# When the token numbers are written, and when the last of eight batches is placed, in a Fourier mixing and mixture-of-experts kernel

## The chip, the cores and the metric

The kernel runs on one core of a Trainium2 chip. Its time is the device time of one execution in microseconds, given as the median of three runs. The engines are PE (matrix products), DVE (vector work), ACT (activations and copies), POOL (GpSimd, which here mainly issues the indirect DMAs) and SP, which issues plain loads.

## What is computed

The input is x, 8 batches of 2496 rows of 256 numbers. Each batch is filtered along its rows in the frequency domain; then each of the 19968 rows goes to one of 8 experts, chosen by its logits, and through that expert's two matrices.

```
X = np.fft.rfft(x, axis=1)
F = (filt_r + 1j * filt_i)[None, :, :]
Y = X * F
y = np.fft.irfft(Y, n=x.shape[1], axis=1)
...
logits = x @ w_gate + modality_bias[modality_id]
e_idx = np.argmax(logits, axis=1)
...
for e in range(E):
    mask = e_idx == e
    ...
    h = np.maximum(x[mask] @ w1[e], 0.0)
    out[mask] = gate_w[mask, None] * (h @ w2[e])
```

## The kernel before

The transforms are products with small constant matrices, in three stages for each batch. Stage 3 leaves a batch's filtered rows in an SBUF buffer, yo, as 20 columns (NY) of 128 rows. There are two such buffers (yws, used by batch number modulo 2), so batch g overwrites what batch g-2 left. A row has 256 half-precision numbers, then its token number, then its gate weight.

Routing a batch has four steps. `counting` (line 605) finds each row's expert and counts them, c. `placing` (line 630) writes the token numbers into yo on POOL (line 635), turns the counts into offsets with two matmuls into psO (lines 637 and 638), and computes each row's position, pos_i (line 652). `scatter` (line 674) sends one column of 128 rows to those positions in a DRAM array, bins_d, by an indirect DMA from POOL (line 678): 20 for each batch. `tabling` (line 694) makes the list of blocks of 256 rows of one expert that can now be loaded.

An expert block is loaded by SP (xs, line 756), transposed on PE (pT, line 785) and copied to xT on DVE (line 786). Its expert's w1 is copied on DVE (line 777). Four steps follow, each with a quarter of the first product (line 799, evicted by ACT at line 804) and, for the block before, a quarter of the second (line 812). Then DVE multiplies by the gate weight into osb (line 819; three buffers), and two indirect DMAs from POOL send osb to the rows of out (line 821).

The main loop (line 1136) runs over slots, n. In a slot each batch under way gets a piece of its stages; then `pace` sends some scatters; then expert steps run. Up to slot `end` (87) there are 1.5 steps in a slot; after it, when no stage work is left, four, so one whole block. The last batch's rows are placed in slot 87. The two scatters of an odd slot, and the one of an even slot, become `pace((n - end) % 3)` behind slot 87: one in two of three slots.

PE, ACT and DVE follow a scheduled order that is fixed before the run, and so do the queues of POOL and SP: what stands at a queue's head holds up all behind it. `paced` (line 130) makes an instruction wait for the last matmul in the list marks["pe"] at that point in the program, and so keeps it from being put early in its queue.

Of the kernel before, what the change touches and what calls it, by code (L numbers as in the profile page):

```python
# [16 lines left out]
ALU = mybir.AluOpType  # L17
# [12 lines left out]
def kernel(  # L30
# [12 lines left out]
    nc = tc.nc  # L43

    B, S, D = x.shape
# [31 lines left out]
    DW = D // 2  # L77
# [52 lines left out]
    def paced(ins):  # L130
        tc.add_manual_dep(ins.ins, marks["pe"][-1].name,
                          mybir.DependencyInfo(mybir.DependencyClass.Sync, mybir.DependencyReason.DATA),
                          reason="pace")
# [18 lines left out]
    op = ctx.enter_context(tc.tile_pool(name="opsum", bufs=1, space=bass.MemoryType.PSUM))  # L152
# [34 lines left out]
    NPY = NY // EV  # L187
# [36 lines left out]
    def input_piece(g, k):  # L224

        stage1(g, k)
        if (k + 1) * EV in [t1 for t0, t1 in TCH]:
            load_x()
# [227 lines left out]
    def load_t2(g, c):  # L456
        src = b1_d[g].rearrange("t (jr s) c -> (t jr) s c", jr=4)
        t2 = bp.tile([KB, SCH, D], BF16, tag="t24", name="t2")
        nc.sync.dma_start(t2, src[:, c * SCH:(c + 1) * SCH, :])
        st[g]["t2", c] = t2  # L460

    def load_t4(g, c):
        t0, t1 = TCH[c]
        src = b2_d[g].rearrange("s (jr t) c -> (s jr) t c", jr=4)
        t4 = bp.tile([KA, TCM, D], BF16, tag="t24", name="t4")
        nc.sync.dma_start(t4[:, 0:t1 - t0, :], src[:, t0:t1, :])
        st[g]["t4", c] = t4
# [64 lines left out]
    def stage2(g, k):  # L532

        if k < NK:
            ps = forward(g, k)
        if k > 0:
            pz = inverse(g, k - 1)
        if k < NK:
            filtering(g, k, taken(g, k, ps))
        if k > 0:  # L540
            returned(g, k - 1, pz)
# [88 lines left out]
    def placing(g):  # L630

        yw, lg = st[g]["yw"], st[g]["lg"]
        b3 = [P, NY, E]
        mx, ohT, sc, c = st[g]["route"]
        nc.gpsimd.tensor_single_scalar(yw[:, :, DW:DW + 1], tok, g * S, op=ALU.add)
        psO = pp.tile([P, 2, E], F32, tag="ps")
        nc.tensor.matmul(psO[:, 0, :], lhsT=Lexcl, rhs=c, start=True, stop=True)
        nc.tensor.matmul(psO[:, 1, :], lhsT=ones_sq, rhs=c, start=True, stop=True)
        nc.vector.tensor_sub(lg, lg, mx[:, :, None].to_broadcast(b3))
        nc.scalar.activation(lg, lg, AF.Exp)  # L640
        off = sp.tile([P, E], F32, tag="off")
        nc.vector.tensor_add(off, cnt, ecap)
        nc.vector.tensor_add(off, off, psO[:, 0, :])
        nc.vector.tensor_add(cnt, cnt, psO[:, 1, :])
        yield
        nc.vector.tensor_add(sc, sc, off[:, :, None].to_broadcast([P, E, NY]))
        nc.vector.tensor_mul(sc, sc, ohT)
        yield
        pos = sp.tile([P, NY], F32, tag="pos")
        nc.vector.reduce_sum(pos, sc.rearrange("p e t -> p t e"), axis=AX.X)  # L650
        pos_i = sp.tile([P, NY], I32, tag="posi", bufs=2)
        nc.vector.tensor_copy(pos_i, pos)
        st[g]["pos"] = pos_i
        yield
        ssum = sp.tile([P, NY], F32, tag="ssum")
        nc.vector.reduce_sum(ssum, lg, axis=AX.X)
        nc.vector.reciprocal(yw[:, :, DW + 1].bitcast(F32), ssum)
# [6 lines left out]
    def count(g):  # L664

        run(counting(g))

    def place(g):

        run(placing(g))  # L670
# [3 lines left out]
    def scatter(g, t):  # L674

        rows = P if t < NYF else KA
        with behind("out", 1):
            ins = nc.gpsimd.indirect_dma_start(  # L678
                out=bins_d[:, :], out_offset=IOA(ap=st[g]["pos"][:rows, t:t + 1], axis=0),
                in_=st[g]["yw"][:rows, t, :], in_offset=None)  # L680

        free_of(ins, "bins")
        free_of(ins, "bin_reads")
        tc.add_to_no_dep_group("bins", ins.ins)
        written.append(ins.ins)
        paced(ins)
# [141 lines left out]
    def pad_bins():  # L828

        end = tp_.tile([P, E], F32, tag="end")  # L830
        nc.vector.tensor_add(end, cnt, ecap)
        end_i = tp_.tile([P, E], I32, tag="endi")
        ts(end_i, end, 1.0, 1.0)
        for e in range(E):
            r = nc.values_load(end_i[0:1, e:e + 1], engines=(ET.SP,), min_val=0, max_val=E * CAP - BLK)
            ins = nc.sync.dma_start(bins_d[ds(r, BLK)].rearrange("(p i) w -> p i w", i=NI), pad)
            free_of(ins, "bins")
            free_of(ins, "bin_reads")
            tc.add_to_no_dep_group("bins", ins.ins)
# [61 lines left out]
    opening = []  # L901
    moe = Experts()
    to_bins = []
# [12 lines left out]
    def pace(left):  # L916

        if to_bins and left:
            g, t = to_bins[0]
            if t < NY:  # L920
                scatter(g, t)
                to_bins[0][1] += 1
                left -= 1
            else:
                if g == B - 1:
                    pad_bins()
                opening.append((g, n))
                to_bins.pop(0)
        return left


    def routed(g):

        place(g)
        to_bins.append([g, 0])

    def tabled(g):

        run(tabling(g, KR[g], g == B - 1))
# [8 lines left out]
    with tc.manual_schedule(engines={ET.PE, ET.Activation, ET.DVE}):  # L948
# [92 lines left out]
        tok = const_pool.tile([P, NY, 1], I32)  # L1041
# [36 lines left out]
        def routes(g):  # L1078

            yield from counting(g)  # L1080
            for _ in range(4):
                yield
            yield from placing(g)
            to_bins.append([g, 0])
            yield
            yield from tabling(g, KR[g], False)
# [19 lines left out]
        n = -LONG  # L1106
# [22 lines left out]
    end = begin[B - 1] + OFF3 + NPY + 3  # L1129
    assert opening and not to_bins  # L1130
    n = opening[0][1] + WAIT
# [1 line left out]
    for b in moe.ready:  # L1133
        b["slot"] = 1
    n = 0
    while n <= end or to_bins or opening:
        if n == 0:
            routed(TURNED - 1)
        if n == 4:
            tabled(TURNED - 1)  # L1140
        for g in range(TURNED + 2, B):
            if 0 <= n - begin[g] < NP:
                input_piece(g, n - begin[g])
        for g in range(TURNED + 1, B):
            k = n - begin[g] - OFF2
            if (k + LEAD) % 4 == 0 and 0 <= k + LEAD < NS // EV:
                load_t2(g, (k + LEAD) // 4)
            if 0 <= k <= NS // EV:
                stage2(g, k)
        for g in range(TURNED, B):  # L1150
            k = n - begin[g] - OFF3
            if (k + LEAD) % 3 == 0 and 0 <= k + LEAD < NPY:
                load_t4(g, (k + LEAD) // 3)
            if 0 <= k <= NPY + 1:
                stage3(g, k)
            if k == NPY + 2:
                count(g)
            if k == NPY + 3:
                routed(g)
                tabled(g)  # L1160
        if n <= end:
            pace(pace(pace(3) if n < 8 else 2) if n % 2 or n < GAP else 1)
            owed += STEPS
        else:
            pace((n - end) % 3)
            owed += FT // FQ
        while owed >= 1:
            owed -= 1
            moe.step()
        n += 1  # L1170
# [43 lines left out]
```

## Time and profile before

| | before |
|---|---|
| median of three runs | 594.89 us (594.38 to 596.47) |
| the profiled execution | 592.98 us, with a span of 591.2 us |
| mean granted TensorE clock | 0.941 of full speed |
| share of the span: PE, DVE, ACT, POOL | 87%, 64%, 64%, 62% |

The span is the part of the execution from the first to the last instruction of the profile; all times below count from its start. A busy share is an average over stages that have different limits.

### The profile page before, as it was taken

The numbers are of one execution on the slowest core, as the hardware profiler recorded it, in microseconds if no ns is written. First come the engines' busy times: TensorE is split into PE (matmuls) and PEld (weight loads), VectorE is DVE, ScalarE is ACT, GpSimd is POOL, SyncE is SP. The second block draws the span as 40 slices with busy tenths as digits, with TensorE's granted clock in tenths as the row PEclk, the third lists the DMA queues.
The fourth block names the chain that finished last, engine by engine and source line by source line (L and its number), as shares of the span: only waits on it lengthen the run. The fifth ranks groups of instructions, "written<-read, shape, count | busy, mean of one in ns | idle before, by whom it ended". The sixth has DMA issues, their size and how long they took to land.

```text
span 591.2 us, 16242 instructions
## 1 busy us (share of the span) xinstructions
PE 512.1 (87%) x5115; PEld 463.2 (78%) x5115; DVE 377.6 (64%) x1209; ACT 379.9 (64%) x693; POOL 367.4 (62%) x409
## 2 busy tenths in 40 slices
PE   3689986739969989999999989966999999999991
PEld 2677875628858888888888978855999999999991
DVE  8557986656766777769679777554555555555541
ACT  4578886827856877777876754433666666666660
POOL 8112336727746776774776776777777777655552
PEclk9969998969998998999998999978999999999997
DMA  8949999887697787898667463224444443333321
GB/s 152 184 68 192 197 212 208 180 204 209 160 239 208 203 198 222 231 211 241 184 176 204 139 165 112 87 86 146 137 127 123 119 125 122 118 109 110 99 73 33
DMA packets 69301, 93.29 MB, mean 158 GB/s; under 512 B 11427, under 2 KB 52841, under 8 KB 69059
## 3 DMA queue, kind: packets, MB, share of 16 engines
q0 software_dynamic: 21504, 50.75, 35.2%
q1 hardware_dynamic: 24409, 29.94, 20.1%
q10 hardware_dynamic: 23302, 11.50, 7.4%
q8 instruction: 48, 0.79, 0.6%
q14 instruction: 38, 0.31, 0.2%
HBM read 64.68 MB, written 46.35 MB: 188 GB/s over the span
## 4 chain that ended last, share of the span: by engine, by line
PE 46%; DMA 20%; issue 11%; POOL 9%; DVE 8%; ACT 3%; SPq 0%; POOLq 0%; DVEq 0%; ACTq 0%
PE hps L799 14%; PE ops L812 13%; POOL out_dram L821 5%; DMA t<-b_d 5%; DMA b_d<-t 3%; DMA bins_d<-yo,pos_i 3%; DMA b_d<-z 3%; PE ps L476 3%; DMA out_dram<-osb,meta 2%; DMA g<-g 2%; PE pz L488 2%; PE lt L584 2%; PE ps L569 2%; PE pz L489 2%; PE pT L785 2%
## 5 line engine op out<-in xcount | busy, mean ns | idle before, releaser
L804 ACT ACTIVATE hT<-hps 128x512 f16<-128x512 f32 x316 | 188.1, 597 | 120.7 <-PE hps L799 118.7
L799 PE MATMUL hps<-xT,w 128*128 128x256 f16 x1264 | 203.6, 282 | 5.7 <-DVE xT L786 5.6
L821 POOL DMA_INDIRECT out_dram<-osb,meta x158 | 160.1, 1014 | 76.4 <-DVE osb L819 36.6
L812 PE MATMUL ops<-w2sb,hT 128*128 x1264 | 198.5, 277 | 2.7 <-issue 2.5
L678 POOL DMA_INDIRECT bins_d<-yo,pos_i x160 | 162.1, 1013 | 56.6 <-issue 19.8
L799 PEld LDWEIGHTS <-w 128*128 128x128 f16 x1264 | 148.1, 146 | 11.0 <-DVE xT L786 6.0
L812 PEld LDWEIGHTS <-hT 128*128 128x128 f16 x1264 | 125.2, 99 | 18.9 <-issue 3.1
L819 DVE TENSOR_SCALAR osb<-ops,meta 128x256 f32<-128x256 f32 x158 | 69.4, 475 | 24.9 <-DMA out_dram<-osb,meta 17.3
L777 DVE COPY w<-w1sb 128x2048 f16 x79 | 56.2, 711 | 42.9 <-PE hps L799 41.1
L786 DVE COPY xT<-pT 128x512 f16<-128x512 f16 x79 | 33.4, 423 | 53.0 <-PE pT L785 52.3
L503 ACT CAST xf<-ps 104x512 f16<-104x512 f32 x96 | 56.9, 592 | 11.5 <-PE ps L476 9.5
L510 DVE TENSOR_TENSOR p<-xf,g 104x512 f16<-104x512 f16 x96 | 40.5, 421 | 36.7 <-ACT xf L503 35.8
L525 ACT CAST z<-pz 104x512 f16<-104x512 f32 x72 | 42.5, 590 | 9.7 <-PE pz L489 8.1
L476 PE MATMUL ps<-t,w2m 104*104 104x256 f16 x192 | 39.9, 292 | 8.7 <-DMA t<-b_d 7.9
L511 DVE TENSOR_TENSOR xf<-xf,g 104x512 f16<-104x512 f16 x96 | 40.5, 421 | 10.0 <-DMA g<-g 6.9
L488 PE MATMUL pz<-p,a1m 104*104 104x256 f16 x144 | 37.5, 284 | 2.7 <-DVE p L510 1.8
L218 ACT CAST t<-ps 96x512 f16<-96x512 f32 x52 | 30.1, 581 | 14.3 <-PE ps L214 12.8
L593 DVE COPY yT<-lt 128x512 f16<-128x512 f16 x80 | 33.5, 419 | 7.1 <-PE lt L589 6.3
L489 PE MATMUL pz<-xf,a2m 104*104 104x256 f16 x144 | 36.6, 280 | 0.0
L785 PE MATMUL pT<-ident,xs 128*128 128x128 f16 x316 | 32.8, 227 | 4.4 <-DMA xs<-bins_d 4.4
L144 POOL DMA_DIRECT2D xt<-in_x_dram x32 | 18.3, 573 | 28.7 <-PE fp L253 14.2
L584 PE MATMUL lt<-ident,yo 128*128 128x128 f16 x320 | 31.4, 221 | 3.7 <-ACT z L525 3.3
(206 smaller groups left out, 725.5 us busy)
## 6 DMA issues: line engine op xcount, KB each, us to landing
xs<-bins_d SPq DMA_DIRECT2D x79, 130.0 KB
xt<-in_x_dram POOLq DMA_DIRECT2D x24, 384.0 KB
t<-b_d SPq DMA_DIRECT2D x18, 384.0 KB
t<-b_d SPq DMA_DIRECT2D x15, 416.0 KB
b_d<-z ACTq DMA_DIRECT2D x30, 208.0 KB
b_d<-t ACTq DMA_DIRECT2D x24, 192.0 KB
w1sb<-in_moe_w_dram POOLq DMA_DIRECT2D x16, 256.0 KB
w2sb<-in_moe_w_dram POOLq DMA_DIRECT2D x8, 512.0 KB
```

The lines of the kernel that those rows point to most:

```text
L476: mm = nc.tensor.matmul(ps[:KB, i, :], lhsT=w2m[:, s + i, :], rhs=st[g]["t2", s // SCH][:, s % SCH + i, :], start=True, stop=True)
L488: nc.tensor.matmul(pz[:KB, i, :], lhsT=a1m[:, s + i, :], rhs=p1[:, i, :], start=True, stop=False)
L489: nc.tensor.matmul(pz[:KB, i, :], lhsT=a2m[:, s + i, :], rhs=p2[:, i, :], start=False, stop=True)
L503: nc.scalar.copy(xf, ps[:KB])
L678: ins = nc.gpsimd.indirect_dma_start(out=bins_d[:, :], out_offset=IOA(ap=st[g]["pos"][:rows, t:t + 1], axis=0), in_=st[g]["yw"][:rows, t, ...
L777: cp = nc.vector.tensor_copy(b["w1"].rearrange("p a f -> p (a f)"), w1sb[:, ds(ej, 1)].rearrange("p o a f -> p (o a f)"))
L785: nc.tensor.transpose(pT[:, dc, i, :], xh[:, i, dc * P:(dc + 1) * P], ident)
L799: mm = nc.tensor.matmul(hps[:, k, :], lhsT=b["w1"][:, dc, ft:F:FT], rhs=b["xT"][:, dc].rearrange("p i t -> p (i t)"), start=(dc == 0), sto ...
L804: nc.scalar.activation(b["hT"][:, q * FQ:(q + 1) * FQ, :], hps, AF.Relu)
L812: nc.tensor.matmul(b["ops"][:, i, :], lhsT=b["hT"][:, ft, i * P:(i + 1) * P], rhs=w2sb[:, ds(b["ej"], 1), ft, :], start=(ft == 0 and i == ...
L819: nc.vector.tensor_scalar_mul(osb[:, i, :], b["ops"][:, i, :], gate[:, i, :])
L821: ins = nc.gpsimd.indirect_dma_start(out=out[:, :], out_offset=IOA(ap=b["meta"][:, i, 0:1], axis=0), in_=osb[:, i, :], in_offset=None, bou ...
```

## The change

The token-number write of each batch gets the paced wait. The last batch is placed at slot 89, two slots later, and its scatters then go in three of four slots.

```
@@ -632,7 +632,7 @@
         yw, lg = st[g]["yw"], st[g]["lg"]
         b3 = [P, NY, E]
         mx, ohT, sc, c = st[g]["route"]
-        nc.gpsimd.tensor_single_scalar(yw[:, :, DW:DW + 1], tok, g * S, op=ALU.add)
+        paced(nc.gpsimd.tensor_single_scalar(yw[:, :, DW:DW + 1], tok, g * S, op=ALU.add))
@@ -1133,7 +1133,7 @@
     n = 0
-    while n <= end or to_bins or opening:
+    while n <= end + 2 or to_bins or opening:
@@ -1155,14 +1155,14 @@
             if k == NPY + 2:
                 count(g)
-            if k == NPY + 3:
+            if k == NPY + (3 if g < B - 1 else 5):
                 routed(g)
                 tabled(g)
         if n <= end:
             pace(pace(pace(3) if n < 8 else 2) if n % 2 or n < GAP else 1)
             owed += STEPS
         else:
-            pace((n - end) % 3)
+            pace((n - end) % 4)
             owed += FT // FQ
```

The order of instructions on an engine shows what moves. The first place is POOL's queue where the scatters of batch 4 end and those of batch 5 begin. Here yo_105 is the buffer of the even batches and yo_106 that of the odd ones; the names in brackets are what an instruction waits for, DMASW being the software DMAs that POOL issues itself. Before:

```order
L678 DMA bins_d<-yo_105,pos_i 162048x130 [waits DMASW0_49,PE_49,Activation_49]
L678 DMA bins_d<-yo_105,pos_i 162048x130 [waits DMASW1_49]
L635 TENSOR_SCALAR yo_105<-tok 128x20 [waits DMASW3_49,DMASW4_49,DMASW2_49,DMASW7_49,DMASW1_49,DMASW0_49]
L821 DMA out_dram<-osb,meta 19968x256 [waits DVE_49] x2
L678 DMA bins_d<-yo_106,pos_i 162048x130 [waits DVE_49,PE_49,Pool_49]
```

With the change, in the same place:

```order
L678 DMA bins_d<-yo_105,pos_i 162048x130 [waits DMASW0_49,PE_49,Activation_49]
L678 DMA bins_d<-yo_105,pos_i 162048x130 [waits DMASW1_49]
L635 TENSOR_SCALAR yo_106<-tok 128x20 [waits PE_49]
L821 DMA out_dram<-osb,meta 19968x256 [waits DMASW2_49,DVE_49]
L821 DMA out_dram<-osb,meta 19968x256 [waits DMASW3_49,DVE_49]
```

The write that stands there was that of batch 6, into the buffer that the scatters above it read; it is now that of batch 5, into the other buffer. The DMAs behind it get waits of their own for the DMA eight places ahead, which the old write had covered. The same holds for batches 3, 4 and 6.

The second place is POOL's queue from the last scatters of batch 6 (yo_105) to the first of batch 7 (yo_106). Before:

```order
L678 DMA bins_d<-yo_105,pos_i 162048x130 x5
L821 DMA out_dram<-osb,meta 19968x256 x4
L678 DMA bins_d<-yo_106,pos_i 162048x130 x3
L821 DMA out_dram<-osb,meta 19968x256 x2
L678 DMA bins_d<-yo_106,pos_i 162048x130
```

With the change:

```order
L678 DMA bins_d<-yo_105,pos_i 162048x130 x5
L821 DMA out_dram<-osb,meta 19968x256 x4
L635 TENSOR_SCALAR yo_106<-tok 128x20
L821 DMA out_dram<-osb,meta 19968x256 x2
L678 DMA bins_d<-yo_106,pos_i 162048x130
L821 DMA out_dram<-osb,meta 19968x256 x2
L678 DMA bins_d<-yo_106,pos_i 162048x130
```

The write of batch 7 arrives here, from the place ahead of batch 6's scatters, and the three scatters in a row are gone.

The third place is DVE's queue where batch 7 is placed and tabled. Before:

```order
L727 SCALAR_TENSOR_TENSOR bj<-bj,done,jio 128x25
L777 ISA
L777 COPY w_8407<-w1sb 128x2048
L819 TENSOR_SCALAR osb<-ops,meta 128x256 x2
L775 TENSOR_LOAD ej_i
L775 ISA x2
L786 COPY xT<-pT 128x512
```

With the change:

```order
L819 TENSOR_SCALAR osb<-ops,meta 128x256
L725 TENSOR_REDUCE bj<-m 128x25
L819 TENSOR_SCALAR osb<-ops,meta 128x256
L727 SCALAR_TENSOR_TENSOR bj<-bj,done,jio 128x25
L777 ISA
L777 COPY w_8405<-w1sb 128x2048
L775 TENSOR_LOAD ej_i
L775 ISA x2
L786 COPY xT<-pT 128x512
```

The copy of w1 and two steps of the table, which stood ahead of the fourth multiply into osb after the counts, now stand between its halves or behind it. On PE the two psO matmuls move behind one more block; ACT's order stays.

## Rows read from the trace of the kernel before

**Rows 1.** The page, busy time (share of the span) and instructions of each engine.

```profile
PE 512.1 (87%) x5115; PEld 463.2 (78%) x5115; DVE 377.6 (64%) x1209; ACT 379.9 (64%) x693; POOL 367.4 (62%) x409
```

**Rows 2.** Stages: length, busy PE, PEld, DVE, ACT, POOL (instructions), clock, DMA share, GB/s.

```profile
364.00:383.00 19.00, 19.00 (x216) 17.59 (x215) 11.25 (x34) 10.12 (x17) 14.54 (x15) 1.00 0.28 85
383.00:412.00 29.00, 18.54 (x133) 15.23 (x132) 14.64 (x52) 9.07 (x16) 22.03 (x23) 0.82 0.36 112
425.00:507.00 82.00, 82.00 (x790) 77.26 (x789) 44.73 (x111) 52.22 (x88) 63.03 (x62) 1.00 0.42 126
```

**Rows 3.** Waits of DVE from 364 to 430: total us, times, longest.

```profile
DVE osb L819 <- DMA out_dram<-osb,meta: 17.3, 8, 5.5
```

**Rows 4.** Timeline of PE, 380 to 500: start, duration, instruction [idle before <-releaser].

```profile
381.65 0.39 PE L785 MATMUL pT<-ident,xs 128*128 128x128 f16 x4
...
388.80 0.60 PE L637 MATMUL psO<-c,Lexcl 128*128 128x8 f32 x2 [5.33 <-DVE c L627]
...
401.28 0.66 PE L799 MATMUL hps<-xT,w 128*128 128x256 f16 x4 [1.18 <-DVE xT L786]
...
409.37 1.07 PE L799 MATMUL hps<-xT,w 128*128 128x256 f16 x4 [3.94 <-DVE xT L786]
...
425.44 0.38 PE L785 MATMUL pT<-ident,xs 128*128 128x128 f16 x4
...
496.59 0.39 PE L785 MATMUL pT<-ident,xs 128*128 128x128 f16 x4
```

**Rows 5.** Timeline of POOL, 224 to 405, at the token-number writes and a later pair.

```profile
224.38 0.74 POOL L635 TENSOR_SCALAR yo<-tok 128x20 int32<-128x20 int32 x1 [4.36 <-DMA bins_d<-yo,pos_i]
...
268.61 1.05 POOL L678 DMA_INDIRECT bins_d<-yo,pos_i  x1 [0.30 <-PE ps L214]
276.06 0.32 POOL L635 TENSOR_SCALAR yo<-tok 128x20 int32<-128x20 int32 x1 [6.41 <-DMA bins_d<-yo,pos_i]
...
277.47 1.30 POOL L821 DMA_INDIRECT out_dram<-osb,meta  x1 [0.30 <-DVE yT L593]
...
316.63 0.91 POOL L678 DMA_INDIRECT bins_d<-yo,pos_i  x1 [0.30 <-issue]
320.25 0.28 POOL L635 TENSOR_SCALAR yo<-tok 128x20 int32<-128x20 int32 x1 [2.72 <-DMA bins_d<-yo,pos_i]
...
359.51 1.33 POOL L678 DMA_INDIRECT bins_d<-yo,pos_i  x1 [0.30 <-issue]
363.74 0.28 POOL L635 TENSOR_SCALAR yo<-tok 128x20 int32<-128x20 int32 x1 [2.89 <-DMA bins_d<-yo,pos_i]
...
404.07 1.00 POOL L821 DMA_INDIRECT out_dram<-osb,meta  x1 [0.30 <-issue]
```

**Rows 6.** Timeline of DVE: one multiply, and the positions of batches 5 and 6.

```profile
271.66 0.47 DVE L819 TENSOR_SCALAR osb<-ops,meta 128x256 f32<-128x256 f32 x1
...
315.53 0.17 DVE L652 CAST pos_i<-pos 128x20 int32<-128x20 f32 x1
...
355.79 0.17 DVE L652 CAST pos_i<-pos 128x20 int32<-128x20 f32 x1
```

**Rows 7.** Timeline of DVE, 384 to 410.

```profile
384.67 0.88 DVE L819 TENSOR_SCALAR osb<-ops,meta 128x256 f32<-128x256 f32 x2 [4.41 <-DMA out_dram<-osb,meta]
...
401.53 0.31 DVE L727 SCALAR_TENSOR_TENSOR bj<-bj,done,jio 128x25 f32<-128x25 f32 x1
...
407.95 0.88 DVE L819 TENSOR_SCALAR osb<-ops,meta 128x256 f32<-128x256 f32 x2 [5.51 <-DMA out_dram<-osb,meta]
...
409.33 0.68 DVE L777 COPY w<-w1sb 128x2048 f16 x1
```

**Rows 8.** Timelines: POOL's last scatter, SP's load behind it, PE's transposes of that block.

```profile
500.74 0.92 POOL L678 DMA_INDIRECT bins_d<-yo,pos_i  x1 [0.30 <-PE pT L785]
...
503.15 0.33 SPq L756 DMA_DIRECT2D xs<-bins_d  x1
...
519.15 0.39 PE L785 MATMUL pT<-ident,xs 128*128 128x128 f16 x4
```

More of the change, by code (lines that the diff above doesn't have):

```diff
@@ L634, in placing @@
         mx, ohT, sc, c = st[g]["route"]
-        nc.gpsimd.tensor_single_scalar(yw[:, :, DW:DW + 1], tok, g * S, op=ALU.add)
+        paced(nc.gpsimd.tensor_single_scalar(yw[:, :, DW:DW + 1], tok, g * S, op=ALU.add))
         psO = pp.tile([P, 2, E], F32, tag="ps")
@@ L1135 @@
     n = 0
-    while n <= end or to_bins or opening:
+    while n <= end + 2 or to_bins or opening:
         if n == 0:
@@ L1157 @@
                 count(g)
-            if k == NPY + 3:
+            if k == NPY + (3 if g < B - 1 else 5):
                 routed(g)
@@ L1164 @@
         else:
-            pace((n - end) % 3)
+            pace((n - end) % 4)
             owed += FT // FQ
```

## The prediction

> **What bounds the kernel now.** I read the page first, then the stages, then the three engines that meet in the worst stage. The page gives PE 87% of the span and POOL 62% [rows 1]; a mean like this hides that POOL is the limit in one stretch. In the windows, PE is busy for 82 of 82 us from 425 on, but for only 18.5 of 29 us between 383 and 412, with a granted clock of 0.82 there [rows 2]. Just before, from 364 to 383, POOL issues 15 instructions in 19 us, and 23 in the next 29 us: one every 1.26 us, with nothing free between them.
>
> The waits say who holds whom: DVE's multiply into osb (line 819) waits 17.3 us in eight pieces for scatters into out [rows 3]. osb has three buffers, so block k needs the landing of block k-3's two scatters, and those stand in POOL's queue behind the scatters into the bins. PE then waits for what is queued behind line 819 on DVE: 5.33 us for the counts c, later 1.18 and 3.94 us for xT [rows 4].
>
> How much is lost? In the undisturbed part 19 blocks, by their transposes, take 496.59 - 425.44 = 71.15 us, 3.74 us each. The seven blocks from 381.65 to 425.44 take 43.79 us where 7 x 3.74 = 26.2 would do, plus 0.9 for the two psO matmuls: **16.7 us lost** [rows 4]. That is the most that this stretch can give back.
>
> Why is POOL so late? At each token-number write (line 635) it stands still until the scatters just ahead in its own queue have landed: 6.41, 2.72 and 2.89 us before the writes at 276.06, 320.25 and 363.74 [rows 5]. It was reading ahead: the write for batch g stood one batch early, directly behind the last scatters of the buffer that it overwrites.
>
> **The change, part by part.**
>
> *The tied write.* The eight writes stay, 0.3 us each. They now stand just ahead of their own batch's scatters and wait for PE alone, as the first pieces of the order show. By then their buffer's scatters have landed long ago, since stage 3 has overwritten that buffer. So the three stalls go. What POOL finds next decides how much of each is kept:
> - Batch 4. POOL is free of the last scatter at 268.61 + 1.05 = 269.66. The next scatter into out needs osb, which DVE finishes at 271.66 + 0.47 = 272.13 [rows 6]; so it goes out at about 272.5 in place of 277.47 [rows 5]. Kept: 5.0 of the 6.41 us.
> - Batch 5. The last scatter ahead ends at 317.54 [rows 5], now 312.5. The write, two scatters into out (2.6 us) and gaps lead to about 316.2. That batch's positions are ready at 315.53 + 0.17 = 315.7 [rows 6], so POOL doesn't wait for them. Kept: 2.72 less some 0.3 for the write's own gap, 2.4.
> - Batch 6. The same sum: 2.89 less 0.2, and positions are ready at 355.96 [rows 6] against a first scatter near 357. Kept: 2.7.
>
> Together POOL runs 5.0 + 2.4 + 2.7 = **10.1 us earlier** from about 357 on. It does not fall idle in between: the positions come 0.3 to 1 us ahead of it. The paced wait is for a matmul ahead of psO, which the positions need anyway, so it is over earlier still.
>
> There is a new wait to price: in the order each scatter now also waits for the software DMA eight places ahead. The slowest landing seen is from 268.61 to 276.06, 7.45 us [rows 5], and eight places take 8 x 1.26 = 10.1 us. I take nothing; the lower bound is nothing, the upper one the 2.7 us of one short stall.
>
> The Trainium skill, DMA: Bandwidth & Descriptors, section Anatomy of one DMA — SWDGE (gpsimd) path, prices a DMA from this queue at about 2.0 us fixed plus bytes over 436 GB/s. For a scatter of 128 rows of 520 bytes that is an estimate of 2.15 us; three such waits less their gaps would make a lead of 5.6 us, less the 1.3 us below a gain of 4.3, and 590.6 us at the end. The rows above show up to 7.45 us under load, so I keep them.
>
> *Placing two slots later.* PE's two psO matmuls move behind one more block, and with them DVE's steps from line 643 on. The work is the same. Before, PE stood 5.33 us at psO for c [rows 4], because c stood on DVE behind the line 819 that waited for a landing until 384.67 [rows 7]. That landing now comes at 384.67 - 10.1 = 374.6, before DVE needs it near 380.3 (384.67 less its 4.41 us of waiting). So this stall goes through POOL's lead alone, and the move is cover on top. It also carries a cost: in the order of the change DVE's placing and tabling steps crowd around the multiply that is late next. Lines 725, 727 and the w1 copy (line 777) now stand between that multiply and the next xT copy. I take 0.31 us, line 727's, for each of the two steps and 0.68 for the copy [rows 7], 1.3 us in all; nothing is the lower bound.
>
> *Three per four.* Behind the write, batch 7's first three scatters no longer stand in one row ahead of a pair for out; one does. From there on POOL has 11 issues in four blocks (8 out, 3 bins) in place of 8 in three. Between 425 and 507 it issued 62 in 82 us, 1.32 us each [rows 2]: 11 x 1.32 = 14.5 us, against 4 x 3.74 = 14.96 us of PE. It fits, narrowly. Batch 7's last scatter moves one block later, 3.74 us against PE. Before, it is issued at 500.74, the load that waits for it at 503.15, and PE takes up that block at 519.15 [rows 8]: 16 us of cover, some 10 left after the move and a POOL that lags 2 us more. Price nothing; without cover each microsecond late would count in full.
>
> **The sum.** What is late next is the same multiply as before, the one at 407.95 [rows 7], since the pair that frees its buffer stands behind nine bin scatters that the change doesn't move. This pair goes out at 404.07 - 10.1 = 394.0 and lands, 3.88 us after its issue as before, at 397.85. PE would like to go on at 383.5 + 3 x 3.74 + 0.9 = 395.6 (383.5 being half a block behind the transposes at 381.65), so a wait remains. Before, PE resumed at 409.37, 1.42 us behind that multiply's start; now at 397.85 + 1.42 + 1.3 = 400.6. **Gain: 409.37 - 400.6 = 8.8 us.** Behind it the next multiplies are due near 402, 408 and 412. The pairs that they need are issued from 394.0 on at 2.6 us a pair, with the write or one scatter between, and land near 401, 404 and 408. From 509 on nothing changes in size. The half-speed matmuls after the one remaining stall stay in both traces. The profiled execution took 592.98 us; less 8.8 that is 584.2. The median, 594.89, is 1.9 us above it, so I predict 594.89 - 8.8 = **586.1 us**.
>
> **The rivals.** About 0.3% (1.8 us) is what a measurement here can tell from no change.
> - *Everything comes back.* If POOL's lead reached 15 us, no multiply would wait: 594.9 - 16.7 = 578.2. For it: there is also a stall of 4.36 us at 224.38 [rows 5], which I count at nothing, because the work between 225 and 276 had time to absorb it. Against it: the positions of batches 5 and 6 are ready only 0.3 to 1 us before POOL wants them, which caps the lead. Gain over 12 us: chance 0.10.
> - *A smaller lead.* POOL's pitch is 1.26 us while DVE stands waiting and 1.32 us while DVE works [rows 2]. If the freed DVE slows POOL between 357 and 397, 30 issues cost 30 x 0.06 = 1.8 us, and if half of batch 4's gain is lost to pacing, 2.5 more: gain 4.6, time 590.3. The Trainium skill, SBUF — State Buffer, section Who interferes with whom, has a rule that points this way: VectorE and GpSimd share a pair of ports, and a copy in a two-port mode blocks GpSimd's descriptor writing until it ends. Gain 2 to 5 us: chance 0.09.
> - *No effect.* If only the last stall counts, 2.7 less the 1.3 on DVE gives 1.4 us, 593.5: chance 0.08.
> - *Slower: POOL becomes the bound of the tail.* The place is the 22 blocks over which batch 7 is scattered. It decides from a pitch of 14.96 / 11 = 1.36 us on; each 0.1 us above that costs 1.1 us in four blocks, 6 us in all. To end slower than before the pitch must pass 1.36 + (8.8 + 1.8) / 60 = 1.54; at 1.60 the cost is 5.5 x 11 x 0.24 = 14.5 us and the time 594.9 - 8.8 + 14.5 = 600.6. Against it: 1.32 was measured with the same mix. Chance 0.05.
> - That the write does not move is excluded by the order.
>
> **How the numbers follow.** The forecast, a gain of 5 to 12 us, has the remaining 0.68, its own range 583 to 590. The range to hold 8 in 10 runs from inside the first rival to inside the second: 580.5 to 591.5 us. Faster by over 0.3%: 0.68 + 0.10 + 0.09 = 0.87; same 0.08; slower 0.05.
>
> **What would show it.** Right: no idle time of several us before line 635 on POOL; the wait of 5.33 us at psO gone; the scatters of batch 6 start near 357; one stall of PE near 396 to 401, with line 819 waiting for a scatter into out near 397.9; the transposes 3.74 us apart from about 410 to the end. Wrong: POOL idle before line 635 for PE, or before scatters for a software DMA or for positions (then the lead is smaller); a pitch over 1.36 us after 410 with line 819 waiting again; PE waiting for xs near 510. If PE's loss between 380 and 420 is still over 14 us, the step from POOL's lead to the landing is wrong.

## The result, and the profile after

The changed kernel takes 588.1 us, the median of four runs (586.75 to 589.24); the kernel before took 595.47 us in the runs beside it. The ratio is 0.9876, with a 95% interval of 0.9846 to 0.9905: 7.4 us faster, where 8.8 us and 586.1 us were predicted. The profiled execution of after is one of 589.24 us, with a span of 587.4 us.

The page's line of busy times, to be read against [rows 1]:

```profile
PE 507.8 (86%) x5115; PEld 460.9 (78%) x5115; DVE 376.2 (64%) x1209; ACT 379.7 (65%) x693; POOL 370.1 (63%) x409
```

Nothing in it has moved by more than a point. The windows of the same stretches as in [rows 2] say more (columns as there):

```profile
364.00:383.00 19.00, 19.00 (x223) 17.69 (x222) 13.09 (x44) 10.15 (x17) 14.65 (x15) 1.00 0.28 85
383.00:412.00 29.00, 24.11 (x217) 21.56 (x215) 16.89 (x60) 14.06 (x25) 22.58 (x23) 0.94 0.41 132
...
425.00:507.00 82.00, 82.00 (x789) 77.09 (x787) 44.89 (x111) 52.11 (x88) 63.23 (x62) 1.00 0.40 123
```

Between 383 and 412 PE now issues 217 instructions where it issued 133, with a granted clock of 0.94 in place of 0.82. POOL's 23 issues are the same: it is as full as before, but it is further on in its list. (Batch 6's psO comes 4.3 us later in this trace, as shown below; a window moved by as much, 387.3 to 416.3, has PE busy for the same 24.11 us.) The total of DVE's waits for scatters into out, to be read against [rows 3], falls from 17.3 us in eight pieces to this:

```profile
DVE osb L819 <- DMA out_dram<-osb,meta: 5.7, 2, 4.5
```

The timeline of POOL at the token-number writes and at what follows them, against [rows 5]:

```profile
273.70 0.29 POOL L635 TENSOR_SCALAR yo<-tok 128x20 int32<-128x20 int32 x1
...
276.37 1.06 POOL L821 DMA_INDIRECT out_dram<-osb,meta  x1 [2.38 <-DVE ni L705]
277.74 1.07 POOL L678 DMA_INDIRECT bins_d<-yo,pos_i  x1 [0.30 <-issue]
...
315.93 0.35 POOL L635 TENSOR_SCALAR yo<-tok 128x20 int32<-128x20 int32 x1
...
321.40 0.98 POOL L678 DMA_INDIRECT bins_d<-yo,pos_i  x1 [1.95 <-issue]
...
358.39 0.28 POOL L635 TENSOR_SCALAR yo<-tok 128x20 int32<-128x20 int32 x1
...
361.47 0.98 POOL L678 DMA_INDIRECT bins_d<-yo,pos_i  x1 [0.31 <-PE ps L572]
...
398.73 1.00 POOL L821 DMA_INDIRECT out_dram<-osb,meta  x1 [0.30 <-DVE m L723]
400.04 0.99 POOL L821 DMA_INDIRECT out_dram<-osb,meta  x1 [0.30 <-issue]
...
499.37 0.91 POOL L678 DMA_INDIRECT bins_d<-yo,pos_i  x1 [0.30 <-PE hps L799]
```

None of these writes has idle time ahead of it. Two earlier ones, of batches 0 and 2, have, 1.50 us at 83.23 and 3.03 us at 166.86, both for PE, which the prediction had named as a sign of a smaller lead; but the scatter into out behind the second goes out at 167.68, and before it went out at 168.55. Two short idle times stand elsewhere, 2.38 us before a scatter into out and 1.95 us before batch 5's first scatter. DVE's timeline shows what they are for:

```profile
275.61 0.48 DVE L819 TENSOR_SCALAR osb<-ops,meta 128x256 f32<-128x256 f32 x1
...
320.45 0.17 DVE L652 CAST pos_i<-pos 128x20 int32<-128x20 f32 x1
```

The first is the wait for osb that the prediction counted: the multiply ends at 276.09. For the second the profile names no releaser, but that scatter reads batch 5's positions, and these are ready at 320.62, 0.78 us before it starts. In the second trace of the changed kernel, reported below, it again starts 0.78 us behind them (315.96 to 316.74, with 1.87 us idle). The rows at 398.73 and 400.04 are the pair that [rows 5] shows with its first half at 404.07. PE, against [rows 4]:

```profile
355.15 0.39 PE L637 MATMUL psO<-c,Lexcl 128*128 128x8 f32 x2 [0.78 <-DVE c L627]
...
397.12 0.66 PE L799 MATMUL hps<-xT,w 128*128 128x256 f16 x4 [0.91 <-DVE xT L786]
...
405.22 1.07 PE L799 MATMUL hps<-xT,w 128*128 128x256 f16 x4 [3.98 <-DVE xT L786]
...
408.41 0.39 PE L785 MATMUL pT<-ident,xs 128*128 128x128 f16 x4
412.14 0.38 PE L785 MATMUL pT<-ident,xs 128*128 128x128 f16 x4
...
498.31 0.38 PE L785 MATMUL pT<-ident,xs 128*128 128x128 f16 x4
```

The 5.33 us at batch 7's psO are gone. One stall of 3.98 us remains, with 0.91 us a block ahead of it. From 408.41 on the transposes stand 3.75 us apart: 24 blocks take 89.90 us. The timeline of DVE at the two multiplies that still wait, against [rows 7]:

```profile
393.67 0.88 DVE L819 TENSOR_SCALAR osb<-ops,meta 128x256 f32<-128x256 f32 x2 [1.24 <-DMA out_dram<-osb,meta]
...
402.90 0.48 DVE L819 TENSOR_SCALAR osb<-ops,meta 128x256 f32<-128x256 f32 x1 [4.46 <-DMA out_dram<-osb,meta]
```

**A measure that compares executions.** Absolute times don't compare well here: batch 6's psO starts at 350.83 in the trace before and at 355.15 after. Most of what follows is read from the **stretch**, the time from the start of that psO to the end of the span, and from two points counted from the same psO: the **pair**, the first of the four scatters into out behind batch 6's last five (398.73 above), and the **restart** of PE behind its longest late stall (405.22 above). The **lead** is how much earlier the pair stands than in the two executions of before, 52.6 us on average. All columns but the last are from one profiled execution in each row.

| kernel | span | psO of batch 6 | stretch | pair | lead | time, or ratio to before |
|---|---|---|---|---|---|---|
| before | 591.2 | 350.83 | 240.4 | 53.2 | | 595.47 |
| before again | 586.9 | 346.41 | 240.5 | 52.0 | | 588.76 (one run) |
| after | 587.4 | 355.15 | 232.3 | 43.6 | 9.0 | 0.9876 [0.9846, 0.9905] |
| after again | 580.5 | 350.52 | 230.0 | 43.1 | 9.5 | 582.36 (one run) |
| write tied only | 585.6 | 350.66 | 234.9 | 44.4 | 8.2 | 0.9908 [0.9869, 0.9947] |
| placing and cadence only | 591.7 | 350.87 | 240.8 | 52.6 | 0.0 | 1.0009 [0.9975, 1.0043] |
| changed, write tied in batch 5 only | 590.1 | 352.12 | 238.0 | 51.5 | 1.1 | 591.97 (one run) |
| changed, write tied in 6 and 7 only | 584.7 | 351.58 | 233.1 | 46.4 | 6.2 | 586.54 (one run) |
| tied and later, old cadence | 588.6 | 352.79 | 235.8 | 45.0 | 7.6 | 0.981 [0.9733, 0.9887] |
| before, four osb | 587.3 | 347.45 | 239.9 | 56.9 | -4.3 | 0.9979 [0.9944, 1.0014] |
| after, four osb | 578.3 | 348.11 | 230.2 | 44.9 | 7.7 | 0.9707 [0.963, 0.9783] |

The ratios leave out the slower of a kernel's executions where they spread: the one of "after, four osb" rests on three of six runs and the one of the old cadence on two of four, and the traces of the old cadence and of the changed kernel on the slower chip (below) are of executions that are left out.

### The profile page after: what moved, and what is told of

Same layout as the page of the kernel before. It is cut to its first block, busy times and chain, and to the rows that moved or that the text cites. A ratio compares the mean times of both kernels' runs of the same rounds, so it can differ in the third digit from the quotient of the medians.

```text
span 587.4 us, 16253 instructions
## 1 busy us (share of the span) xinstructions
PE 507.8 (86%) x5115; PEld 460.9 (78%) x5115; DVE 376.2 (64%) x1209; ACT 379.7 (65%) x693; POOL 370.1 (63%) x409
## 4 chain that ended last, share of the span: by engine, by line
PE 51%; DMA 17%; issue 10%; DVE 8%; POOL 7%; ACT 4%; SPq 1%; DVEq 0%; POOLq 0%; ACTq 0%
PE hps L799 16%; PE ops L812 15%; DMA b_d<-t 5%; POOL out_dram L821 5%; DMA t<-b_d 4%; PE ps L476 2%; PE ps L569 2%; PE lt L584 2%; DMA g<-g 2%; PE pz L488 2%; PE pT L785 2%; PE ps L572 2%; PE pz L489 2%; PE ps L214 1%; DMA g<-in_filt_i_dram 1%
## 5 line engine op out<-in xcount | busy, mean ns | idle before, releaser
L678 POOL DMA_INDIRECT bins_d<-yo,pos_i x160 | 164.4, 1027 | 68.2 <-issue 21.7
L821 POOL DMA_INDIRECT out_dram<-osb,meta x158 | 161.5, 1022 | 71.8 <-DVE osb L819 34.7
L476 PE MATMUL ps<-t,w2m 104*104 104x256 f16 x192 | 39.2, 287 | 10.1 <-DMA t<-b_d 9.3
L569 PE MATMUL ps<-t,wbm 96*128 96x256 f16 x120 | 30.6, 284 | 4.9 <-DMA t<-b_d 4.8
```

The costliest lines, as they stand in the source:

```text
L476: mm = nc.tensor.matmul(ps[:KB, i, :], lhsT=w2m[:, s + i, :], rhs=st[g]["t2", s // SCH][:, s % SCH + i, :], start=True, stop=True)
L678: ins = nc.gpsimd.indirect_dma_start(out=bins_d[:, :], out_offset=IOA(ap=st[g]["pos"][:rows, t:t + 1], axis=0), in_=st[g]["yw"][:rows, t, ...
L821: ins = nc.gpsimd.indirect_dma_start(out=out[:, :], out_offset=IOA(ap=b["meta"][:, i, 0:1], axis=0), in_=osb[:, i, :], in_offset=None, bou ...
```

## The experiments

**The tied write alone.** The first hunk of the change, nothing else.

```
-        nc.gpsimd.tensor_single_scalar(yw[:, :, DW:DW + 1], tok, g * S, op=ALU.add)
+        paced(nc.gpsimd.tensor_single_scalar(yw[:, :, DW:DW + 1], tok, g * S, op=ALU.add))
```

> Only the token-number write is tied to its placing; the last batch is placed where it was, at two scatters in three blocks. Theory (POOL's lead does it): the three standstills of POOL before line 635 go, the 5.33 us wait at psO shrinks to under 1 us although psO has not moved, and nearly the whole gain is here: 588 us, 586.5 to 590. Rival (the later placing does it, as cover for the counts): the stall at psO stays at 3 us or more and the time is 593 to 596.

Measured: 587.25 us against 593.27. Its timeline of PE shows four idle pieces between 380 and 420:

```profile
383.76 0.39 PE L637 MATMUL psO<-c,Lexcl 128*128 128x8 f32 x2 [0.99 <-DVE c L627]
...
393.43 0.66 PE L799 MATMUL hps<-xT,w 128*128 128x256 f16 x4 [1.22 <-DVE xT L786]
...
401.08 1.07 PE L799 MATMUL hps<-xT,w 128*128 128x256 f16 x4 [3.43 <-DVE xT L786]
...
416.09 0.66 PE L799 MATMUL hps<-xT,w 128*128 128x256 f16 x4 [1.72 <-DVE xT L786]
```

The psO wait shrinks from 5.33 to 0.99 us without the later placing. So it does go through POOL's lead. The last piece, 1.72 us, is one that after doesn't have; it comes after the three scatters of batch 7 in one row.

**The later placing and the new cadence, without the tied write.**

```
-    while n <= end or to_bins or opening:
+    while n <= end + 2 or to_bins or opening:
...
-            if k == NPY + 3:
+            if k == NPY + (3 if g < B - 1 else 5):
...
-            pace((n - end) % 3)
+            pace((n - end) % 4)
```

> Only the last batch's placing two slots later, and three scatters in four blocks; the write is not tied. Theory: the 5.33 us wait at psO goes, but PE then waits for the same multiply into osb, whose buffer is freed at about 408 as before; POOL still stands still before line 635; time 594.5 us, 593 to 596. Rival (later placing does it): 588 to 590 us.

Measured: no difference, 593.46 us against 593.27. POOL's timeline still has the idle time before its writes; three rows of it, and PE's two longest stalls:

```profile
274.68 0.33 POOL L635 TENSOR_SCALAR yo<-tok 128x20 int32<-128x20 int32 x1 [6.56 <-DMA bins_d<-yo,pos_i]
...
319.33 0.34 POOL L635 TENSOR_SCALAR yo<-tok 128x20 int32<-128x20 int32 x1 [4.00 <-DMA bins_d<-yo,pos_i]
...
363.39 0.52 POOL L635 TENSOR_SCALAR yo<-tok 128x20 int32<-128x20 int32 x1 [2.50 <-DMA bins_d<-yo,pos_i]
```

```profile
388.43 1.07 PE L799 MATMUL hps<-xT,w 128*128 128x256 f16 x4 [4.60 <-DVE xT L786]
...
401.89 1.07 PE L799 MATMUL hps<-xT,w 128*128 128x256 f16 x4 [4.00 <-DVE xT L786]
```

The 5.33 us have left psO, which now stands one block further on, and come back as 4.60 us for xT. Placing later moves the wait; it doesn't shorten it.

**Both kernels again**, unchanged, to see how much one execution differs from the next.

> The changed kernel once more, for a second profile. Its first profile has 4.3 us more of waiting ahead of batch 6's psO than the kernel before (loads t from b_d, 5.71 and 3.57 us). Theory (these waits differ from run to run): psO of batch 6 anywhere from 350 to 355.5, with other single waits for t. Rival (the tied write brings them): the waits for t near 178 and 231 come again within 0.5 us each and psO of batch 6 is at 354.5 to 355.8.

> The kernel before once more, for a second profile. Theory: psO of batch 6 between 350 and 355, so that part of the difference in the profiles is between runs; the stalls at 383 to 409 come again within 1 us each. Rival: psO of batch 6 at 350.8 within 0.5 us.

Measured: stretches of 230.0 and 240.5 us, so the stretch of before repeats within 0.2 us and that of after within 2.3. What lies ahead does not repeat: batch 6's psO starts at 346.41 in the second trace of before, outside what was expected of it either way, and at 350.83 in the first. The difference is there early. The first psO behind 60 us starts at 84.19 and 78.20 us in the two traces of before, at 84.29 and 82.87 in those of after. In the second trace of before PE's stalls are 5.47 us at psO and the one below for xT (5.33 and 3.94 in the first); the piece of 1.18 us doesn't come again.

```profile
403.68 0.79 PE L799 MATMUL hps<-xT,w 128*128 128x256 f16 x4 [3.76 <-DVE xT L786]
```

The second trace of after has its two stalls, 1.36 and 3.83 us, where the first has 0.91 and 3.98:

```profile
350.52 0.39 PE L637 MATMUL psO<-c,Lexcl 128*128 128x8 f32 x2 [0.76 <-DVE c L627]
...
392.05 0.66 PE L799 MATMUL hps<-xT,w 128*128 128x256 f16 x4 [1.36 <-DVE xT L786]
...
400.00 0.66 PE L799 MATMUL hps<-xT,w 128*128 128x256 f16 x4 [3.83 <-DVE xT L786]
```

Of the two early waits for t, the one of 5.71 us near 178 comes again as 5.14 us and the one near 231 doesn't. Traces in which batch 2's write isn't tied have 2.16 to 7.05 us near 178, so the tie isn't shown to bring it.

**Four osb buffers in place of three**, in the kernel before and in the changed one. To make room, xs has four in place of five.

```
-        xs = ep.tile([P, NI, RW], I32, tag="xs", bufs=5)
+        xs = ep.tile([P, NI, RW], I32, tag="xs", bufs=4)
...
-            osb = ep.tile([P, NI, D], F32, tag="osb", bufs=3)
+            osb = ep.tile([P, NI, D], F32, tag="osb", bufs=4)
```

> The kernel before with a fourth buffer for osb, and to make room one buffer less for xs (four). The measure beside the time is the stretch from batch 6's psO to the end of the span: 240.4 and 240.5 us in two profiles of the kernel before. Theory (PE is held by POOL's lateness through the ring of osb): one more buffer lets a multiply wait for a pair one block earlier, so POOL may be one block later, 3.7 us, and no more, because POOL's own queue is as late as before: stretch 236 to 237.5, 3 to 4 us less. Rival 1 (it is the ring alone that is too short): the stalls go, stretch 224 to 228. Rival 2 (the counts and the placing hold PE): 240 to 241, as before.

> The changed kernel with four buffers for osb and four for xs. Its stretch from batch 6's psO to the end was 232.3 and 230.0 us in two profiles, with stalls of 0.9 to 1.4 and 3.8 to 4.0 us. Theory: with POOL's lead of some 10 us the fourth buffer covers what is left; no wait for xT over 1 us between 380 and 420; stretch 223.5 to 226 and about 6 us less time than the change, 581 to 583 on a chip where the kernel before takes 594. Rival (what remains is the w1 copy and the table's steps on DVE, or the two slots' worth of placing): the stall of 3.8 us stays, 587 to 589.

Both missed in the stretch: 239.9 and 230.2 us, no shorter than with three buffers. With the change, the multiply one block further on waits, and for the same pair. DVE's and PE's timelines show it:

```profile
397.77 0.88 DVE L819 TENSOR_SCALAR osb<-ops,meta 128x256 f32<-128x256 f32 x2 [7.06 <-DMA out_dram<-osb,meta]
```

```profile
399.07 1.07 PE L799 MATMUL hps<-xT,w 128*128 128x256 f16 x4 [5.12 <-DVE xT L786]
```

In the kernel before, PE's one wait at psO became 0.95 us and five pieces of 1.61 to 2.77 us followed, since POOL's pair stood at 56.9, 4.3 us later still. A buffer more lets DVE run one block further ahead; it doesn't bring the pair forward. Yet the changed kernel with four osb buffers took 580.62 us against 593.29, which is 0.979 by these medians and 0.9707 by the table, both below the change itself. Its trace has nothing of this in the stretch; batch 6's psO comes earlier, at 348.11 against 355.15 and 350.52, but it moves by as much between executions of one kernel. So the cause stays open. Both pools were changed at once, so none of this is shown for the fourth osb buffer alone.

**The tied write in some batches only**, in the changed kernel, so with its later placing and cadence, which alone give no lead. Batch 5 alone (the idle time of 6.41 us at 276.06 goes), then batches 6 and 7 (those of 2.72 and 2.89 us go).

```
+        (paced if g == 5 else id)(nc.gpsimd.tensor_single_scalar(...))
```

```
+        (paced if g >= 6 else id)(nc.gpsimd.tensor_single_scalar(...))
```

> The change, but only batch 5's write is tied; that takes away the longest standstill of POOL, 6.41 us before 276, and leaves the ones before 320 and 364. Theory (POOL's lead is what counts, wherever it comes from): some 5 us of lead, stretch from batch 6's psO to the end about half way between the late placing alone (240.8) and the change (230.0 to 232.3): 235 to 237.5. Rival (only the standstills near the stalls count, an early one is made up): 239.5 to 241.

> The change, but only the writes of batches 6 and 7 are tied; that takes away the standstills of 2.72 and 2.89 us before 320 and 364 and leaves the one of 6.41 us before 276. Theory (POOL's lead counts, and adds up): some 5 us of lead, stretch from batch 6's psO to the end 235 to 237.5, like the run with batch 5 alone. Rival (only the standstills near the stalls count): the whole gain, 230 to 232.5.

Measured: stretches of 238.0 and 233.1 us, leads of 1.1 and 6.2 us. Each stretch lies between what the theory and the rival had, so neither holds as it was put. In the first, POOL's next writes stand still for longer at 319.13 and for nearly as long at 363.24; in the second the 6.29 us at 276.16 remain:

```profile
319.13 0.81 POOL L635 TENSOR_SCALAR yo<-tok 128x20 int32<-128x20 int32 x2 [4.50 <-DMA bins_d<-yo,pos_i]
...
363.24 0.45 POOL L635 TENSOR_SCALAR yo<-tok 128x20 int32<-128x20 int32 x1 [2.56 <-DMA bins_d<-yo,pos_i]
```

```profile
276.16 0.29 POOL L635 TENSOR_SCALAR yo<-tok 128x20 int32<-128x20 int32 x1 [6.29 <-DMA bins_d<-yo,pos_i]
...
357.40 0.29 POOL L635 TENSOR_SCALAR yo<-tok 128x20 int32<-128x20 int32 x1
```

In these single executions the longest of the three idle times is worth the least. Of the 6.41 us, 0.5 to 1.8 came back as a longer wait at the next write (4.50 us, for 2.72 in before and 4.00 with nothing tied and the later placing), and 1.1 is all that reached the pair. The two short ones nearest to the stall, 5.6 us together, gave 6.2.

**The changed kernel, the one with four osb buffers, and one with four xs buffers alone, on one chip.** This chip turned out to take some 20% longer for every kernel, the one before included (719.1 us).

> The changed kernel once more, now on the same chip as the two versions below. Theory: its time stands at 0.985 to 0.991 of the kernel before (about 587 to 588 us of 593 to 595); the stretch from the start of batch 6's positions to the end of the span is 229.5 to 232.5 us, and its one stall of PE of 3 to 4.5 us stands 41 to 43 us behind that start. Rival: the first comparison was helped by what lies ahead of batch 6's positions (350.5 and 355.2 us in two executions, 346.4 and 350.8 before); then the ratio lies at 0.993 or above, with the stretch unchanged.

> The changed kernel with four osb buffers and four of xs, again. Theory A (the fourth osb buffer only moves the stall one block on): the time is within 0.5% of the changed kernel's, 585 to 590 us, stretch 229 to 232 us, and the 580.6 us of the first time came from an early part of 343 to 349 us that this chip gives the changed kernel as well. Theory B (the version is truly faster): 578 to 583 us, over 0.7% below the changed kernel on the same chip, with batch 6's positions at 347 to 349 us where the changed kernel has 350 to 355; then it is the part ahead of batch 6 that differs, and not the stall.

> The changed kernel with four xs buffers in place of five and osb left at three. Theory A: no difference to the changed kernel beyond 0.5%, 585 to 590 us; its stall stands where the changed kernel has it, 41 to 43 us behind the start of batch 6's positions, 3 to 4.5 us long. Theory B, if four osb buffers with four xs are truly faster: a time like theirs (578 to 583 us) says that the smaller xs pool, or where it puts the later buffers, does it; a time like the changed kernel's says that the fourth osb buffer does.

Measured: 712.04, 708.63 and 711.95 us; ratios to before of 0.9938 [0.9888, 0.9989], 0.986 [0.9814, 0.9905] and 0.9911 [0.9864, 0.9959]. None of the expected times and stretches applies (the stretches are 284.5, 282.1 and 284.9 us). The four osb buffers are again the lowest, but the intervals of all three meet, so which of the two edits helps, and whether by more than some tenths of a per cent, stays open. The trace of the changed kernel shows what is different here: in the window from 500 to 560 PE has a granted clock of 1.00 and is yet busy for 50.31 of 60 us.

```profile
500.00:560.00 60.00, 50.31 (x439) 43.53 (x438) 25.39 (x64) 28.38 (x50) 32.53 (x34) 1.00 0.34 103
```

```profile
567.96 0.60 PE L799 MATMUL hps<-xT,w 128*128 128x256 f16 x4 [0.52 <-issue]
568.75 0.69 PE L812 MATMUL ops<-w2sb,hT 128*128 x4 [0.20 <-issue]
569.28 0.38 PE L785 MATMUL pT<-ident,xs 128*128 128x128 f16 x4
...
574.20 0.39 PE L785 MATMUL pT<-ident,xs 128*128 128x128 f16 x4
```

PE stands for parts of a microsecond within a block, waiting for nothing that the profile shows, and a block takes 574.20 - 569.28 = 4.92 us in place of 3.74. POOL waits for DVE's multiply in this trace, and DVE's multiply waits for no scatter into out at all (such a row is missing among its waits). POOL's total of waits:

```profile
POOL out_dram L821 <- DVE osb L819: 107.2, 59, 9.9
```

In after that total is 34.7 us. With slow blocks POOL keeps up, and PE has no stall that a scatter into out ends; it does have one of 4.55 us at 480.08, put down to ACT (line 804). This fits a gain of only 0.6%, though its interval meets that of the first measurement; the kernel before wasn't profiled on this chip, so that its stall is smaller there too is argued, not shown.

**The tied write and the later placing, with the old cadence.**

```
-            pace((n - end) % 4)
+            pace((n - end) % 3)
```

> The tied write and the placing two slots later, with the scatters of batch 7 at two per three blocks as before. It leaves out only the new cadence, to see which of the two gives the 2.7 to 5 us of stretch that the whole change has over the tied write alone (stretch from the start of batch 6's positions to the end of the span: 234.9 us with the tied write alone, 232.3 and 230.0 with the whole change). Theory A (the later placing does it, because it keeps three scatters in one row from standing ahead of a pair for out): the stretch is 229.5 to 232.5 us, one stall of PE of 3 to 4.5 us 41 to 43 us behind batch 6's positions and none near 65 us. Theory B (the cadence does it): the stretch is 234 to 237 us, with a second or third stall behind 50 us. Should this run fall on the chip that took 712 us for the changed kernel, neither can be told.

Measured: 588.37 us against 594.87, and a stretch of 235.8 us, where theory B had it: in this trace the later placing adds nothing without the new cadence. The times don't tell: the ratio, 0.981 from two runs and 0.989 by the medians of all, has an interval that meets those of the whole change and of the tied write alone. PE's stalls are 4.73, 1.40 and 0.79 us, and it stands again near the end. POOL's last scatter into the bins, and PE around 516:

```profile
510.62 1.28 POOL L678 DMA_INDIRECT bins_d<-yo,pos_i  x1 [0.30 <-PE hps L799]
```

```profile
516.33 0.39 PE L785 MATMUL pT<-ident,xs 128*128 128x128 f16 x4 [0.27 <-issue]
517.36 1.03 PE L799 MATMUL hps<-xT,w 128*128 128x256 f16 x8 [0.64 <-DVE xT L786]
...
521.66 0.67 PE L812 MATMUL ops<-w2sb,hT 128*128 x4 [0.42 <-issue]
```

The last scatter goes out at 510.62, against 499.37 with the new cadence, and PE loses 0.27 + 0.64 + 0.42 = 1.3 us when it comes to the block that needs it. That is the cover which the prediction counted: the load of that block waits for the last scatter, and PE for the load. But not all 3.6 us against after are the cadence's: the pair was already 1.4 us later (45.0 against 43.6), and its place in POOL's queue lies ahead of the first scatter that the cadence moves.

## Why the prediction was right, step by step

**POOL's lead: right.** 10.1 us were predicted, 9.0 and 9.5 measured. POOL's waits for landings before line 635 are gone with the tied write alone. The first scatter of batch 6, predicted near 357, stands at 361.47 in a trace that is 4.3 us late at psO, and at 356.83 in the other.

**How the lead adds up: right in the sum, too high for batch 5.** POOL's timeline before, at the first scatters of batches 4, 5 and 6:

```profile
279.07 0.97 POOL L678 DMA_INDIRECT bins_d<-yo,pos_i  x1 [0.30 <-PE ps L476]
...
323.65 0.97 POOL L678 DMA_INDIRECT bins_d<-yo,pos_i  x1 [0.30 <-PE pT L785]
...
367.13 0.98 POOL L678 DMA_INDIRECT bins_d<-yo,pos_i  x1 [0.30 <-PE lt L589]
...
405.37 0.98 POOL L821 DMA_INDIRECT out_dram<-osb,meta  x1 [0.30 <-issue]
```

After, they stand at 277.74, 321.40 and 361.47. Counted from batch 6's psO in each trace they are 5.7, 6.6 and 10.0 us earlier (5.3, 6.5 and 8.9 in the second traces); the prediction had 5.0, 7.4 and 10.1. So batch 4's part held. Batch 5's was 0.9 and 1.2 us in place of 2.4: the step "POOL doesn't wait for them" failed, since batch 5's positions, ready at 320.62, came behind POOL, which was free at 321.40 - 1.95 = 319.45. Batch 6's part was 3.4 and 2.4 us for 2.7. That the sum came out within about 1 us is in part luck.

Nor does each part hold by itself. With batch 5's write alone tied the lead at the pair is 1.1 us, and with the other two 6.2 where 2.4 + 2.7 = 5.1 were counted. The parts make 7.3 apart and 9.0 to 9.5 together, in executions whose pair differs by 1.2 us between the two traces of before. This fits that they help one another: as long as a later write waits for landings, time won ahead of it is partly spent there.

The multiply that waits for the pair starts 2.86 us behind the issue of the pair's second half in the trace after (400.04 to 402.90), and 2.58 us in the one before (405.37 to 407.95 [rows 7]); counted from the first half, as the prediction did, it is 4.17 and 3.88 us. The prediction's estimate of 2.15 us for a DMA with 520-byte rows, and the lead of 5.6 us by it, came from the Trainium skill, DMA: Bandwidth & Descriptors, section Anatomy of one DMA — SWDGE (gpsimd) path. For the 1 KB rows of these scatters the same rule makes an estimate of 2.30 us; both times here are longer than that, and the measured lead is greater than 5.6 us.

**From the lead to the restart: right.** The restart was predicted at 400.6, which is 49.8 us behind batch 6's psO in the trace before. It came at 50.1 and 49.5; before it stood at 58.5 and, in the second trace, 57.3.

**DVE's crowded steps: right in kind, 0.9 for 1.3 us.** PE restarts 2.32 us behind the start of the late multiply (402.90 to 405.22); before it was 1.42 (407.95 to 409.37). Lines 725 and 727 and the w1 copy do stand in between.

**The wait at psO goes through POOL's lead: right.** The tied write alone takes it from 5.33 to 0.99 us; the later placing alone turns it into 4.60 us for xT.

**The later placing and the cadence at nothing: right alone, slightly too low together.** Alone they give a ratio of 1.0009. On top of the tied write the traces suggest that they avoid two losses, each seen in one trace: 1.72 us behind the three scatters in a row, and, since the later placing would use up the cover at the end, the 1.3 us at 516 that the new cadence takes back. The whole change has a stretch 2.7 to 5.0 us shorter than the tied write alone; but two executions of the whole change differ by 2.3 us, and the intervals of the ratios meet. So the size of this part isn't settled, only that it is small beside the tied write's.

**POOL as the bound of the tail: didn't come.** From 425 to 507 POOL issues 62 instructions as before and PE is busy for 82.00 us. A POOL slowed by a busier DVE, which the second rival counted at 1.8 us, doesn't show either: the 28 scatters from batch 6's first to the pair take 37.26 us after (361.47 to 398.73) and 36.94 before (367.13 to 404.07). From 364 to 383 DVE is busy for 13.09 us in place of 11.25, and POOL's 15 instructions take 14.65 us in place of 14.54. The Trainium skill has VectorE and GpSimd share ports in SBUF — State Buffer, section Who interferes with whom; no row here shows an effect of it beyond those tenths of a microsecond.

**The sum.** 8.8 us were predicted for the stretch; 8.1 and 10.4 were measured, and 7.4 in the medians. The time is 2.0 us above the forecast of 586.1, with 0.6 us of that because before, too, measured 595.47 in place of 594.89. The remaining 1.4 us are less than the 4.4 and 4.6 us by which the part ahead of batch 6 differs between two executions of one kernel. One term has no row as it stands: the two psO matmuls, taken at 0.9 us, are 0.60 us long in [rows 4]; it enters only the 16.7 us lost and the 395.6 at which PE would like to go on, not the forecast.

## What to carry to other kernels

An instruction that an in-order queue reaches too early costs more than its own wait: all behind it is late, and the wait for it may show two engines away, as POOL's did on PE by way of DVE. Tie it to something that is sure to be over when its turn comes, and do so at every such place at once, since here one removed wait was partly spent at the next. Then ask what the engine finds next: the lead stops where its data aren't ready, as at batch 5's positions. Before a stall is bought off with a buffer or a later step, look which issue ends it: neither a fourth osb buffer nor the later placing brought that issue forward, and in the traces the wait only moved by a block.

## What the runs showed of the hardware

One chip took 712 us for what takes 588 elsewhere, at a granted clock of 1.00 from 500 to 560 (0.90 over the span, against 0.94), with PE standing inside its blocks for no wait that the profile shows; there the same change was worth 0.6%, with an interval of 0.1 to 1.1% that meets the one of the first measurement. So it isn't settled that the change gives less there.

Two executions of the kernel before differ by 6.0 us already at their first psO behind 60 us (84.19 and 78.20) and by 4.4 us at batch 6's, and then agree within 0.2 us over the last 240. What sets the early part wasn't found.
